# Two attention layers on one core: VectorE takes one head of two tiles per block instead of both heads of one

## The chip, the cores and the metric

The kernel runs on one core of one Trainium2 chip. The metric is the device time of one execution in microseconds. Three runs of the kernel before gave 1418.83, 1418.96 and 1419.97, median 1418.96. The profile shown is of another single execution of it, which took 1422.47 us; its span, from the first to the last instruction, is 1420.7 us.

## The reference

Two independent attention layers over 2048 tokens of width 576, with 32 heads of 18 elements each; their outputs are joined side by side.

```python
# A: one key and one value head for all 32 query heads
q = (x @ wq) as [H, S, 18];  k = x @ wk;  v = x @ wv
p = softmax(einsum("bhqd,bkd->bhqk", q, k) * 18 ** -0.5)
out_A = heads_joined(einsum("bhqk,bkd->bhqd", p, v)) @ wo

# B: per head, 4 segments of 512 tokens, causal within a segment, and a memory
for s in range(4):
    a_dot = softmax(qs @ ks.T * 18 ** -0.5 + causal) @ vs
    a_mem = (phi(qs) @ M) / (phi(qs) @ z + 1e-6)
    o = g * a_mem + (1 - g) * a_dot
    M, z = M + phi(ks).T @ vs, z + sum(phi(ks))
out_B = heads_joined(o) @ wo
```

All of A's scores are needed: 32 heads x 2048 queries x 2048 keys, so some 134 million exponentials. B has the lower triangle of 512 x 512 for each of its 4 segments and 32 heads.

## The kernel before

A first stage makes the projections of both layers, B's memory and an upper bound for each row of scores, and leaves them in DRAM. It ends about 290 us into the span. A second stage is the attention, which this change touches. A tail finishes the last output projections.

**Blocks, items, pairs.** The attention works on blocks. A block of A is 512 queries (chunk `c`) of four heads (`hg`), against all 2048 keys, as 16 key tiles `kt` of 128; a block of B is four heads in one segment, as three groups of key tiles. The four heads are two pairs `pr`. The unit of work, called a tile or an item here, is one key tile of one pair: scores of 128 keys by 2 heads by 512 queries. There are 32 blocks of A with 32 items each, and 32 blocks of B with 6 items; `after` (L869) says behind which block of A two blocks of B follow, at 13 places for A's next block.

**One item.** `scores` (L905) multiplies on TensorE into a tile `E` of two PSUM banks (three such tiles in rotation). ScalarE takes the exponential of `E` into a tile `P` in SBUF (L936). For the middle item of each turn (`copied`), VectorE first copies `E` to `W` in SBUF (L933), so that `E` is free sooner, and ScalarE reads `W`. `products` (L949) multiplies `P` by the values into `O`, accumulated over the block. Each item has two halves `hf` of 256 queries, each with both pairs.

**Exponentials on VectorE.** For the items in `BY_DVE` (L55), here key tile 0 of pair 1, VectorE makes the exponentials of both heads itself, by `exponentials` (L890): a multiply-add of the scores into an integer whose bits are read as a float (L894), two operations on its bits (L896, L897) into the tiles `n` and `q`, and four multiply-adds of a polynomial (L898 to L901), all 1024 elements wide, into the tile `PD`. The first runs with the scores; the other six wait in a list, `slow`, and one is taken per turn (L1121). A turn in which a block's last products run takes none unless it is due.

**Turns.** The order on TensorE, ScalarE and VectorE is written out by hand (L1086). The items of a block are cut into turns of three (`turns`); 32 items make ten turns of three and one of two, which is the last, turn 10. The half products are cut in the same way into `prods`, with the piece of two at place 8. In turn `k` come, in this order: the scores of turn `k` with the copy to `W`; the exponentials on ScalarE, the middle item last; eight matmuls of filling into `F` (`run_fill`, the output projection of an earlier chunk, L773, or B's memory, L829); one step of `slow` on VectorE; the products of piece `k - 2`; and what is due of the work that ends a chunk (`due`, `finish`). So the piece of two products of before runs in turn 10, the turn of two scores. Turn numbers start again in each block, and pieces 9 and 10 run in turns 0 and 1 of the block that follows. When a block's products end, VectorE copies `O` out (L975).

**Order of products.** `turn_of` (L982) holds for each pair the order in which the key tiles are multiplied. An item of VectorE is put back to the position in `LATE`, here 12 of 0 to 15, so that its exponentials are ready.

Of the kernel before, what the change touches and what calls it, by code (L numbers as in the profile page):

```python
# [8 lines left out]
F32 = mybir.dt.float32  # L9
# [3 lines left out]
U32 = mybir.dt.uint32  # L13
AF = mybir.ActivationFunctionType
# [14 lines left out]
SCALE = DH ** -0.5  # L29
# [3 lines left out]
PBUFS = 9  # L33
# [18 lines left out]
POLY = [1.0925606709321247, 32.334180715292455, 88.7610992882796, 4291.093056129828]  # L52
MANTISSA, ONE_BITS, EXPONENT = 0x7FFFFF, 0x3F800000, 0xFF800000

BY_DVE = ((0, 1),)  # L55
LATE = (12,)
QALL = [(slice(0, 36, 2), 0), (slice(1, 36, 2), 1), (slice(36, 54), 0)]
CA = 618
MZ = 126 + 32
# [15 lines left out]
def attention_pair_kernel(ctx, tc, a_xT, a_w, a_wo, b_xT, b_w, b_wo, b_beta, ident_d, hmask_d, bmask_d, cmask_d, sel_d, zmask_d, selx_d, sely_d, out):  # L75
    nc = tc.nc
# [79 lines left out]
    with ExitStack() as ph:  # L156
# [106 lines left out]
        for c in range(NCH):  # L263
# [34 lines left out]
            for t in TILES:  # L298
# [3 lines left out]
                else:  # L302

                    nm, bufs = ("nd", 2) if c == 1 and t == 4 else ("pj", 4)
# [25 lines left out]
                i = 5 * (c - 2) + TILES.index(t)  # L330
# [74 lines left out]
        for s in range(NSEG):  # L405
# [110 lines left out]
            if not last:  # L516
                e = p2.tile([128, 4, DH], F32, name="ph31")
# [92 lines left out]
    with tc.If(loose > 0, preferred_fallthrough_block=False):  # L610
        with ExitStack() as ph:
# [37 lines left out]
            with tc.For_i(0, H, 1) as h:  # L649
# [5 lines left out]
                for i in range(NKT):  # L655
                    s, j = divmod(i, 4)
                    n = 128 * (j + 1)
# [17 lines left out]
    pp = ctx.enter_context(tc.tile_pool(name="pp", bufs=1))  # L675
# [180 lines left out]
    def run_fill():  # L856

        while fill:
            key, steps = fill[0]
            if next(steps, None) is not None:  # L860
                begun.add(key)
                filled[0] += 1
                return
            fill.pop(0)
# [16 lines left out]
    def load_vseg(s):  # L881
        v = pa.tile([128, 4, H * VW + 13], F32, name="vseg", bufs=1)
        nc.sync.dma_start(v[:, :, : H * VW], vB[s].rearrange("(i p) c -> p i c", p=128))
        nc.gpsimd.memset(v[:, :, H * VW :], 0.0)
        vseg[s] = v


    slow, now = [], [0]

    def exponentials(p, e):  # L890

        y, u, w = p.bitcast(U32), pp.tile([128, 2, 512], F32, name="n", bufs=1), pp.tile([128, 2, 512], F32, name="q", bufs=1)
        v, stt = nc.vector, nc.vector.scalar_tensor_tensor
        v.tensor_scalar(y, e, EXP_A, EXP_B, op0=ALU.mult, op1=ALU.add)  # L894
        steps = [
            lambda: v.tensor_scalar(u.bitcast(U32), y, MANTISSA, ONE_BITS, op0=ALU.bitwise_and, op1=ALU.bitwise_or),  # L896
            lambda: v.tensor_scalar(w.bitcast(U32), y, EXPONENT, None, op0=ALU.bitwise_and),  # L897
            lambda: stt(p, u, POLY[0], u, op0=ALU.add, op1=ALU.mult),  # L898
            lambda: stt(p, p, POLY[1], u, op0=ALU.add, op1=ALU.mult),
            lambda: stt(p, p, POLY[2], p, op0=ALU.add, op1=ALU.mult),  # L900
            lambda: stt(p, p, POLY[3], w, op0=ALU.add, op1=ALU.mult),  # L901
        ]
        slow.extend((now[0] + 2 + i, p, step) for i, step in enumerate(steps))

    def scores(it, pr, copied):  # L905

        ab, c, hg, kt = it
        st = stacks[ab, c, hg // 2]
        h = 2 * (hg % 2) + pr
        e = psE.tile([128, 2, 512], F32, name="E")  # L910
        dve = ab == "A" and (kt, pr) in BY_DVE
        p = pp.tile([128, 2, 512], F32, name="PD" if dve else "P", bufs=1 if dve else PBUFS)
        state[it, pr] = p
        n = 512 if ab == "A" else 512 - 128 * kt if kt < 2 else 384
        if ab == "A":
            for j, r0 in enumerate(HALF):
                rows = slice(r0, r0 + KR)
                nc.tensor.matmul(e[:, j], kstA[rows, 128 * kt : 128 * kt + 128], st[rows, h, :], start=True, stop=True)  # L918
            if (kt, pr) in BY_DVE:
                exponentials(p, e)  # L920
                return lambda: None
        else:
            for k, c0 in BKEYS[kt]:
                ks = slice(128 * k, 128 * k + 128)
                for j, r0 in enumerate(HALF):
                    rows = slice(r0, r0 + KR)
                    nc.tensor.matmul(  # L927
                        e[:, j, c0 : c0 + 512 - 128 * k], st[rows, 4 + h, ks], st[rows, h, 128 * k :], start=True, stop=True
                    )
        src = e  # L930
        if copied:
            src = pp.tile([128, 2, 512], F32, name="W", bufs=2)
            nc.vector.tensor_copy(src[:, :, :n], e[:, :, :n])  # L933

        def exponential():
            nc.scalar.activation(p[:, :, :n], src[:, :, :n], AF.Exp, scale=SCALE)  # L936
            if ab == "B":

                m = len(BKEYS[kt])
                diag = p.rearrange("p a (b t) -> p a b t", t=256)[:, :, 0:m, 0:128]  # L940
                nc.gpsimd.affine_select(  # L941
                    diag, diag, pattern=[[0, 2], [0, m], [1, 128]], base=0, channel_multiplier=-1, compare_op=ALU.is_ge, fill=0.0
                )

        return exponential
# [3 lines left out]
    def products(b, m, hf):  # L949


        ab, c, hg = b
        if m == hf == 0:
            acc[0] = psO.tile([128, C], F32, name="O")
        o = acc[0]
        last = (NKT - 1 if ab == "A" else 2) == m
        for j in range(4):
            kt = turn_of[j // 2][m] if ab == "A" else m
            p = state[b + (kt,), j // 2]
            assert all(x[1] is not p for x in slow)  # L960
            k, p0, q0, n = (kt, 256 * hf, 256 * hf, 256) if ab == "A" else BHALF[kt][hf]
            if ab == "A":
                v = VA[:, VW * kt : VW * kt + 32]
            else:
                v = vseg[c][:, k, VW * (4 * hg + j) : VW * (4 * hg + j) + 32]
            nc.tensor.matmul(  # L966
                o[32 * j : 32 * j + 32, q0 : q0 + n],
                v,
                p[:, j % 2, p0 : p0 + n],
                start=m == hf == 0,  # L970
                stop=last and hf == 1,
            )
        if last and hf:
            osb = pa.tile([128, C], F32, name="oe", bufs=4)
            nc.vector.tensor_copy(osb, o)  # L975
            od = oA if ab == "A" else oB
            nc.sync.dma_start(od[c][4 * hg : 4 * hg + 4].rearrange("h r t -> (h r) t"), osb)
            return hg
        return None
# [3 lines left out]
    for pr in range(2):  # L983
        ks = [kt for kt in range(NKT) if (kt, pr) not in BY_DVE]
        for (kt, p_), pos in zip(BY_DVE, LATE):
            if p_ == pr:
# [20 lines left out]
    turns, prods = [], []  # L1007
# [71 lines left out]
    def split(n, cut):  # L1079

        sizes = [3] * (n // 3)
        if n % 3:
            sizes.insert(cut, n % 3)
        return [sum(sizes[:i]) for i in range(len(sizes) + 1)]

    with tc.manual_schedule(engines={ENG.PE, ENG.Activation, ENG.DVE}):  # L1086
# [3 lines left out]
        for n, b in enumerate(blocks):  # L1090
            ms = [m for m in range(len(its)) if block_of[m] == n]
            items = [(m, k) for m in ms for k in range(2)]
            for out_, cut in ((turns, len(items) // 3), (prods, len(items) // 3 - 2)):
                at_ = split(len(items), cut)
                out_ += [items[a:z] for a, z in zip(at_, at_[1:])]
        at(ASK + 4, 0, lambda: True, lambda k: load_qf(2))
# [13 lines left out]
        for k in range(len(turns) + 2):  # L1110
            now[0] = k
            exps = [scores(its[n], pr, i == 1) for i, (n, pr) in enumerate(turns[k])] if k < len(turns) else []
            for i in (0, 2, 1) if len(exps) == 3 else range(len(exps)):
                exps[i]()
            if memory is None:
                run_fill()
            elif k >= ASK and all(its[n][0] == "A" for n, pr in turns[k]) and next(memory, None) is None:
                memory = None

            ends = k > 1 and any(hf and its[n][3] == (NKT - 1 if its[n][0] == "A" else 2) for n, hf in prods[k - 2])  # L1120
            if slow and (slow[0][0] <= k or not ends):  # L1121
                slow.pop(0)[2]()
            for n, hf in prods[k - 2] if k > 1 else []:
                ab, c = its[n][:2]
                hg = products(its[n][:3], its[n][3], hf)
                if hg in (6, 7):
                    finish(k, ab, c, hg)
                if hg == 7 and ab == "B" and c + 1 < NSEG:
                    load_vseg(c + 1)
            due(k)  # L1130
            if k == len(turns):
                halve_w(0)
            for n, pr in turns[k] if k < len(turns) else []:
                it = its[n]
                ab = it[0]
                if pr == 0:
                    prefetch(ab, keys[ab].index((ab, it[1], it[2] // 2)) + 2)
                    if it in (("A", 0, 2, 8), ("A", 0, 5, 8)):
                        load_wo(*(("B", b_wo) if it[2] == 2 else ("A", a_wo)))
# [122 lines left out]
```

## Time and profile before

| | us |
|---|---|
| median of three runs (1418.83 to 1419.97) | 1418.96 |
| the profiled execution | 1422.47 |
| its span | 1420.7 |
| TensorE busy | 1404.0 |
| ScalarE busy | 1205.4 |
| VectorE busy | 964.4 |
| GpSimd (POOL) busy | 244.6 |

In the profile, PE is TensorE's matmuls, PEld its weight loads, ACT ScalarE, DVE VectorE, POOL GpSimd and SP the engine that issues most transfers. A row of a group gives line, engine, operation, what it writes and reads, shapes and count, then the group's busy time in us, the mean of one in ns, and after the second bar the engine's idle time just before these instructions with what ended it. A row of the timeline gives start and length in us, and in brackets an idle time and its releaser. The ends of matmuls are modelled, so that a TensorE that is held back may still count as busy. Successive instructions of ScalarE and VectorE overlap in their records; the distance from start to start is what one costs.

### The profile page before, as it was taken

How to read it: one execution, taken by the hardware profiler on the slowest of the kernel's cores; microseconds unless marked ns; L12 is line 12 of the kernel's file. 1: busy time of each engine (PE TensorE's matmuls, PEld its weight loads, DVE VectorE, ACT ScalarE, POOL GpSimd, SP SyncE). 2: the span in 40 equal slices, each digit the busy share in tenths (PEclk: the TensorE clock that was granted, in tenths of full speed). 3: DMA queues.
4: the chain of work that ended last, by engine and by line, in shares of the span. 5: the costliest groups of instructions: out<-in, count | busy, mean ns of one | idle time of the engine just before them, and what ended most of it. 6: DMA issues, size and time to landing. Idle time of an engine off the chain costs nothing.

```text
span 1420.7 us, 39951 instructions
## 1 busy us (share of the span) xinstructions
PE 1404.0 (99%) x17132; PEld 843.3 (59%) x17132; DVE 964.4 (68%) x1157; ACT 1205.4 (85%) x1447; POOL 244.6 (17%) x326
## 2 busy tenths in 40 slices
PE   9999999999999999999999999999999999999998
PEld 6788888745555555555555555555555555555558
DVE  6656456456677767776766777666767766777663
ACT  4543434479999999999999999999999999999991
POOL 2431000003313213221110160131011400100002
PEclk9999999999999999999999999999999999999999
DMA  9766546557564535332312543232104221110013
GB/s 283 253 216 188 166 146 214 174 171 214 156 214 159 165 120 166 91 109 77 110 58 70 166 128 92 62 107 80 51 34 132 67 76 44 60 45 18 9 59 112
DMA packets 90720, 172.63 MB, mean 122 GB/s; under 512 B 14576, under 2 KB 22889, under 8 KB 90110
## 3 DMA queue, kind: packets, MB, share of 16 engines
q1 hardware_dynamic: 84122, 160.01, 36.0%
q0 software_dynamic: 1664, 4.78, 1.3%
q10 hardware_dynamic: 4752, 5.24, 1.1%
q8 instruction: 135, 2.21, 0.7%
q14 instruction: 47, 0.39, 0.1%
HBM read 99.32 MB, written 70.67 MB: 120 GB/s over the span
## 4 chain that ended last, share of the span: by engine, by line
PE 68%; ACT 7%; issue 2%; DMA 1%; DVE 1%; SPq 0%; ACTq 0%; DVEq 0%
PE O L966 31%; PE E L918 20%; PE F L773 11%; ACT P L936 7%; PE E L927 3%; PE E L1163 2%; PE F L829 1%; DMA stB<-qB 0%; DVE W L933 0%; PE F L1163 0%; PE O L1163 0%; DMA oA<-oe 0%; DMA stB<-kB 0%; DMA sm<-oA 0%; SPq L696 0%
## 5 line engine op out<-in xcount | busy, mean ns | idle before, releaser
L936 ACT ACTIVATE P<-E 128x1024 f32<-128x1024 f32 (+1 forms) x800 | 780.8, 1059 | 12.7 <-PE E L918 12.3
L933 DVE COPY W<-E 128x1024 f32<-128x1024 f32 (+1 forms) x384 | 461.2, 1201 | 248.8 <-PE E L918 189.2
L966 PE MATMUL O<-P,VA 128*32 128x256 f32 x7936 | 508.8, 380 | 0.0
L936 ACT ACTIVATE P<-W 128x1024 f32<-128x1024 f32 (+1 forms) x384 | 426.3, 1110 | 3.4 <-DVE W L933 3.2
L966 PEld LDWEIGHTS O<-P,VA 128*32 128x32 f32 x7936 | 262.2, 110 | 147.6 <-issue 6.6
L918 PE MATMUL E<-stA,kstA 56*128 56x512 f32 x1920 | 329.4, 439 | 1.8 <-DVE W L933 1.1
L918 PEld LDWEIGHTS E<-stA,kstA 56*128 56x128 f32 x1920 | 154.7, 184 | 178.2 <-ACT P L936 113.7
L941 POOL TENSOR_SCALAR_AFFINE_SELECT P<-P 128x256 f32<-128x256 f32 (+1 forms) x192 | 95.0, 495 | 480.3 <-ACT P L936 446.9
L761 POOL TENSOR_TENSOR o<-o,rb 126x512 f32<-126x512 f32 (+1 forms) x55 | 79.9, 1468 | 408.9 <-DMA o<-oA 146.0
L773 PE MATMUL F<-woB,o 126*32 126x192 f32 (+1 forms) x1920 | 127.4, 338 | 0.3 <-DVE osb L797 0.3
L966 PE MATMUL O<-P,vseg 128*32 128x256 f32 (+2 forms) x1536 | 81.8, 344 | 0.8 <-issue 0.8
L773 PEld LDWEIGHTS F<-woB,o 126*32 126x32 f32 (+1 forms) x1920 | 38.2, 108 | 70.6 <-issue 63.6
L975 DVE COPY oe<-O 128x512 f32<-128x512 f32 x64 | 44.3, 692 | 41.8 <-PE O L966 41.0
L252 PE MATMUL pj<-xh,wBl 128*126 128x512 f32 x180 | 72.4, 403 | 0.0
L252 PE MATMUL pj<-xh,wBh 128*126 128x512 f32 x180 | 71.9, 400 | 0.0
L121 ACT CAST qp<-pj 126x512 fp32r<-126x512 f32 (+1 forms) x54 | 31.0, 585 | 46.1 <-DVE kmB L450 32.4
L966 PEld LDWEIGHTS O<-P,vseg 128*32 128x32 f32 x1536 | 49.1, 109 | 25.4 <-issue 2.9
L773 PE MATMUL F<-woA,o 126*32 126x192 f32 (+1 forms) x960 | 63.9, 338 | 0.0
L927 PE MATMUL E<-stB 56*128 56x256 f32 (+3 forms) x512 | 61.3, 347 | 1.4 <-ACT P L936 0.9
L122 DVE TENSOR_TENSOR qp<-pj,qp 126x512 fp32r<-126x512 f32 (+1 forms) x54 | 36.7, 685 | 35.6 <-ACT qp L121 35.3
L252 PE MATMUL pj<-xl,wBh 128*126 128x512 f32 x144 | 57.3, 399 | 0.0
L927 PEld LDWEIGHTS E<-stB 56*128 56x128 f32 x512 | 38.6, 185 | 31.1 <-ACT P L936 20.8
(194 smaller groups left out, 1387.8 us busy)
## 6 DMA issues: line engine op xcount, KB each, us to landing
stB<-kB SPq DMA_DIRECT2D x96, 144.0 KB
stB<-qB SPq DMA_DIRECT2D x32, 288.0 KB
stA<-qA SPq DMA_DIRECT2D x30, 288.0 KB
oA<-oe SPq DMA_DIRECT2D x32, 256.0 KB
oB<-oe SPq DMA_DIRECT2D x32, 256.0 KB
qA<-qp SPq DMA_DIRECT2D x16, 504.0 KB
kB<-qp SPq DMA_DIRECT2D x16, 504.0 KB
qB<-qp SPq DMA_DIRECT2D x16, 504.0 KB
```

The source lines that it names most:

```text
L121: hold(nc.scalar.copy(qp[:R, 0, :n], src))
L122: hold(nc.vector.tensor_tensor(qp[:R, 1, :n], src, qp[:R, 0, :n].bitcast(F32), op=ALU.subtract))
L252: nc.tensor.matmul(dst, w[:, c0 : c0 + M], x, start=i == 0, stop=i == len(ops) - 1)
L761: return lambda: tc.keep_in_program_order(nc.gpsimd.tensor_tensor(dst, a, b, op=op))
L773: nc.tensor.matmul(dst[32 * j : 32 * j + 32], parts[ab, c][: RT[t], t, r0 : r0 + 32], wo[ab][: RT[t], t, c0 : c0 + n], start=start, stop=stop,
L918: nc.tensor.matmul(e[:, j], kstA[rows, 128 * kt : 128 * kt + 128], st[rows, h, :], start=True, stop=True)
L927: nc.tensor.matmul(e[:, j, c0 : c0 + 512 - 128 * k], st[rows, 4 + h, ks], st[rows, h, 128 * k :], start=True, stop=True)
L933: nc.vector.tensor_copy(src[:, :, :n], e[:, :, :n])
L936: nc.scalar.activation(p[:, :, :n], src[:, :, :n], AF.Exp, scale=SCALE)
L941: nc.gpsimd.affine_select(diag, diag, pattern=[[0, 2], [0, m], [1, 128]], base=0, channel_multiplier=-1, compare_op=ALU.is_ge, fill=0.0)
L966: nc.tensor.matmul(o[32 * j : 32 * j + 32, q0 : q0 + n], v, p[:, j % 2, p0 : p0 + n], start=m == hf == 0, stop=last and hf == 1,)
L975: nc.vector.tensor_copy(osb, o)
```

## The change

`BY_DVE` names two items per block of A, key tile 0 of pair 1 (turn 0) and key tile 5 of pair 0 (turn 3). Both are middle items of their turns. Of each, VectorE makes the exponentials of the first head only, with the same seven operations, 512 wide; the second head it copies to `W`, and ScalarE takes a 512-wide exponential of it. The six steps behind the first operation are grouped in three pairs, and a pair is taken per turn. `PD` has two buffers in place of one; `n` and `q` are half as wide. The two items' products stand at positions 7 (pair 1) and 12 (pair 0). The piece of two products moves from place 8 to place 9, so that it runs in turn 0 of the block that follows.

```diff
-BY_DVE = ((0, 1),)
-LATE = (12,)
+BY_DVE = ((0, 1), (5, 0))
+LATE = (7, 12)
...
-    def exponentials(p, e):
-
-        y, u, w = p.bitcast(U32), pp.tile([128, 2, 512], F32, name="n", bufs=1), pp.tile([128, 2, 512], F32, name="q", bufs=1)
-        v, stt = nc.vector, nc.vector.scalar_tensor_tensor
+    def exponentials(p, e, whole):
+
+        u, w = (pp.tile([128, 512], F32, name=nm, bufs=1) for nm in "nq")
+        v, stt, y = nc.vector, nc.vector.scalar_tensor_tensor, p.bitcast(U32)
         v.tensor_scalar(y, e, EXP_A, EXP_B, op0=ALU.mult, op1=ALU.add)
-        steps = [
+        ops = [
...
-        slow.extend((now[0] + 2 + i, p, step) for i, step in enumerate(steps))
+        slow.extend((now[0] + 2 + i, p, ops[2 * i : 2 * i + 2], whole) for i in range(3))
...
-        p = pp.tile([128, 2, 512], F32, name="PD" if dve else "P", bufs=1 if dve else PBUFS)
+        p = pp.tile([128, 2, 512], F32, name="PD" if dve else "P", bufs=2 if dve else PBUFS)
...
-            if (kt, pr) in BY_DVE:
-                exponentials(p, e)
-                return lambda: None
+            if dve:
+                exponentials(p[:, 0], e[:, 0], p)
...
-        src = e
+        src, hs = e, slice(0, 2)
         if copied:
             src = pp.tile([128, 2, 512], F32, name="W", bufs=2)
-            nc.vector.tensor_copy(src[:, :, :n], e[:, :, :n])
+            hs = slice(1, 2) if dve else slice(0, 2)
+            nc.vector.tensor_copy(src[:, hs, :n], e[:, hs, :n])
 
         def exponential():
-            nc.scalar.activation(p[:, :, :n], src[:, :, :n], AF.Exp, scale=SCALE)
+            nc.scalar.activation(p[:, hs, :n], src[:, hs, :n], AF.Exp, scale=SCALE)
...
-            for out_, cut in ((turns, len(items) // 3), (prods, len(items) // 3 - 2)):
+            for out_, cut in ((turns, len(items) // 3), (prods, len(items) // 3 - 1)):
...
-                slow.pop(0)[2]()
+                for op in slow.pop(0)[2]:
+                    op()
```

More of the change, by code (lines that the diff above doesn't have):

```diff
@@ L959, in products @@
             p = state[b + (kt,), j // 2]
-            assert all(x[1] is not p for x in slow)
+            assert all(x[3] is not p for x in slow)
             k, p0, q0, n = (kt, 256 * hf, 256 * hf, 256) if ab == "A" else BHALF[kt][hf]
```

## The prediction

> **What bounds the kernel now.** I read the busy shares first, then the stage after 290 us by blocks, then the wait table, and last the timeline of one block, since two engines stand near full and only the timeline tells which one waits. A block is one run of 16 key tiles by two pairs (32 scored tiles) of A; a turn is three of these tiles.
>
> ```profile
> PE 1404.0 (99%) x17132; PEld 843.3 (59%) x17132; DVE 964.4 (68%) x1157; ACT 1205.4 (85%) x1447; POOL 244.6 (17%) x326
> ...
> ACT  4543434479999999999999999999999999999991
> ...
> PE 68%; ACT 7%; issue 2%; DMA 1%; DVE 1%; SPq 0%; ACTq 0%; DVEq 0%
> ...
> L936 ACT ACTIVATE P<-E 128x1024 f32<-128x1024 f32 (+1 forms) x800 | 780.8, 1059 | 12.7 <-PE E L918 12.3
> ```
>
> TensorE looks full (99%, and 68% of the chain), but the ends of its matmuls are modelled, so that a TensorE that is held back still shows as busy. ScalarE, 85% over the whole span, is at nine tenths or more in every slice of the attention stage. One block late in the stage, in the table by stretches:
>
> ```profile
> core 0: us, PE busy (x) PEld busy (x) DVE busy (x) ACT busy (x) POOL busy (x), PEclk, DMA share, GB/s
> 1204.19:1233.19 29.00, 29.00 (x410) 15.16 (x408) 20.67 (x22) 28.77 (x33) 0.00 (x0) 1.00 0.14 34
> ```
>
> A block takes 29.00 us, of which VectorE works 20.67 and ScalarE 28.77. Where the rest goes, the ScalarE timeline around a block's start shows (the number behind x is the exponentials in the piece):
>
> ```profile
> 1202.34 1.17 ACT L936 ACTIVATE P<-E 128x1024 f32<-128x1024 f32 x1
> 1203.24 1.21 ACT L936 ACTIVATE P<-W 128x1024 f32<-128x1024 f32 x1
> 1204.19 2.10 ACT L936 ACTIVATE P<-E 128x1024 f32<-128x1024 f32 x2
> 1206.52 1.94 ACT L936 ACTIVATE P<-E 128x1024 f32<-128x1024 f32 x2 [0.23 <-PE E L918]
> 1208.34 1.06 ACT L936 ACTIVATE P<-W 128x1024 f32<-128x1024 f32 x1
> 1209.29 1.94 ACT L936 ACTIVATE P<-E 128x1024 f32<-128x1024 f32 x2
> ```
>
> Successive exponentials overlap in the record, so I use start to start: one from E costs (1208.34 - 1206.52)/2 = 0.91, one from the copy W 0.95, a turn of two E and one W 2.76 (1206.52 to 1209.29). The last turn of a block (turn 10) has one E and one W, and turn 0 of the next only two E, since VectorE makes its third: 1.81. But turn 1 starts 2.33 after turn 0: ScalarE loses 0.52 there, 0.23 of it recorded as idle. The other 31 exponentials fill 28.48 of the 29.00, so this is the block's only loss.
>
> TensorE shows why it waits. A turn's order there is scores (E), eight matmuls of filling (F), then the products (O) of two turns earlier:
>
> ```profile
> 1201.12 0.73 PE L918 MATMUL E<-stA,kstA 56*128 56x512 f32 x4
> 1201.78 0.53 PE L773 MATMUL F<-woA,o 126*32 126x192 f32 x8
> ...
> 1203.11 1.18 PE L918 MATMUL E<-stA,kstA 56*128 56x512 f32 x6
> ...
> 1203.56 0.30 PEld L918 LDWEIGHTS E<-stA,kstA 56*128 56x128 f32 x4 [0.27 <-ACT P L936]
> ...
> 1205.98 0.96 PE L918 MATMUL E<-stA,kstA 56*128 56x512 f32 x6
> 1206.86 0.53 PE L773 MATMUL F<-woA,o 126*32 126x192 f32 x8
> ...
> 1208.62 0.96 PE L918 MATMUL E<-stA,kstA 56*128 56x512 f32 x6
> ...
> 1211.28 0.96 PE L918 MATMUL E<-stA,kstA 56*128 56x512 f32 x6
> ```
>
> Unheld, a full turn takes TensorE 2.65 (1208.62 to 1211.28): scores 0.89, filling and three products 1.76. In the short turn, filling and two products took 1.33 (1201.78 to 1203.11), so one product is 0.44 and the filling 0.45. A score matmul that starts at 1205.98 lets ScalarE start at 1206.52, 0.54 later. So in turn 0, where TensorE has a full turn and a score held until its buffer is free (the weight load at 1203.56; 2.87 from 1203.11 to 1205.98) and ScalarE only 1.81 of work, TensorE is late. Everywhere else ScalarE's 2.76 exceeds 2.65 and it is the bound. How often, in the wait table (total, times, longest):
>
> ```profile
> ACT P L936 <- PE E L918: 12.3, 31, 1.8
> ACT P L936 <- DVE W L933: 3.2, 8, 0.9
> ```
>
> 31 waits for 32 blocks; I count 30 of them as this one and the longest, 1.8, as another. Behind a block of B the same wait is larger:
>
> ```profile
> 640.95 0.97 PE L918 MATMUL E<-stA,kstA 56*128 56x512 f32 x6
> ...
> 641.56 1.94 ACT L936 ACTIVATE P<-E 128x1024 f32<-128x1024 f32 x2
> ...
> 643.50 0.96 PE L918 MATMUL E<-stA,kstA 56*128 56x512 f32 x6
> 644.04 1.94 ACT L936 ACTIVATE P<-E 128x1024 f32<-128x1024 f32 x2 [0.55 <-PE E L918]
> ```
>
> 2.48 from turn to turn less 1.81 is 0.67.
>
> **The change, part by part.** *ScalarE.* Two half exponentials from W (one in turn 0, one in turn 3) replace one whole W exponential of turn 3. The trace of before has no half one. Its lower bound is half a whole, 0.47, its upper the whole recorded length of a 512-wide ScalarE instruction, 0.63. I take 0.52, from the 768-wide exponentials of B:
>
> ```profile
> 639.35 1.55 ACT L936 ACTIVATE P<-E 128x768 f32<-128x768 f32 x2
> ...
> 640.73 0.91 ACT L936 ACTIVATE P<-W 128x768 f32<-128x768 f32 x1
> ```
>
> and, among the groups by line,
>
> ```profile
> L389 ACT ACTIVATE ph_e<-ph_e 126x512 f32<-126x512 f32 x28 | 17.7, 632 | 0.7
> ```
>
> A 768-wide one takes 0.69 start to start, 0.215 less than 1024, so 512 less takes 0.43 off 0.95. Per block: 2 x 0.52 - 0.95 = +0.09 (bounds 0 and +0.31).
>
> *Balance.* Turns 0 and 3 cost ScalarE 1.81 + 0.52 = 2.33 each, turn 10 stays 1.86. Before, the 1.86 and 1.81 stood side by side.
>
> *The short product turn* moves one turn on: turn 10 carries one product more on TensorE (+0.44), turn 0 of the next turn list one fewer. No product is added. Where B follows A, it falls into B's first turn in the same way; where A follows B, turn 0 carries B's products and is not shortened. The products of the two tiles that VectorE shares stand at positions 7 and 12; their exponentials end in turns 3 and 6, their first products run in turns 6 and 10, so nothing waits there. No DMA moves, and POOL issues nothing new.
>
> *Putting it together*, block behind block, on the clock of the timeline above. Turn 10's filling starts at 1201.78 as before; filling and three products take 1.76, so turn 0's scores start at 1203.54. They are not held now: the buffer that stopped them came free at 1203.56, before the second score, 0.30 after the first, needs it. Scores 0.89, filling and two products 1.33: turn 1's scores start at 1205.76, and ScalarE can have them at 1206.30. ScalarE does turn 0 from 1204.19 (scores ready 1203.54 + 0.54 = 1204.08, 0.11 to spare) for 2.33 to 1206.52. So turn 1 starts there as before, without a wait, and with half a tile more done. Turns 1 and 2 take 2.76 each, turn 3 from 1212.04 takes 2.33 to 1214.37; TensorE, 2.65 a turn from 1205.76, has turn 4's scores started at 1213.71 and ready at 1214.25, 0.12 to spare. Before, turn 4 started at 1209.29 + 2 x 2.76 = 1214.81. The rest is unchanged: 0.43 less per block (0.52 of wait less 0.09), 28.57 for 29.00.
>
> Behind B, ScalarE would finish turn 0 at 641.56 + 2.33 = 643.89 and the scores come at 644.04 as before: 0.15 of the wait stays, for 13 blocks of 32.
>
> *VectorE.* Seven 1024-wide instructions become fourteen 512-wide, ten whole copies become nine and two halves:
>
> ```profile
> L933 DVE COPY W<-E 128x1024 f32<-128x1024 f32 (+1 forms) x384 | 461.2, 1201 | 248.8 <-PE E L918 189.2 <-PE E L927 47.0 <-ACT P L936 10.6
> ...
> L898 DVE SCALAR_TENSOR_TENSOR PD<-n 128x1024 f32<-128x1024 f32 x32 | 41.5, 1296 | 0.0
> ...
> L797 DVE COPY osb<-F 128x192 f32<-128x192 f32 x72 | 25.0, 347 | 0.3 <-PE F L773 0.3
> ...
> L391 DVE SCALAR_TENSOR_TENSOR qf<-pj,ph_e 126x512 f32<-126x512 f32 x16 | 11.0, 686 | 8.7 <-ACT ph_e L389 8.6
> ```
>
> ```profile
> 1206.82 1.23 DVE L933 COPY W<-E 128x1024 f32<-128x1024 f32 x1 [0.63 <-PE E L918]
> ```
>
> Two halves by the 512-wide row are 2 x 0.69 = 1.37 for a 1024-wide step of 1.30. By the same rows a block's VectorE work grows by some 7 x 0.08 + 0.2 = 0.8 on an engine that works 20.67 of 29.00, so the total is covered. Within a turn it is tighter: copy 1.20 and a pair 1.37 are 2.57 of 2.76; in every fifth turn a copy of 0.35 brings 2.92 by recorded lengths, which overlap a little. The copy may be late by what W's exponential has to spare, about 0.3: it starts 0.84 after its turn's scores (1206.82 less 1205.98), is ready 1.23 later, and its exponential starts 2.36 after the scores (1208.34). Turn 2 had one of the two bit steps there and gets a pair of the dearer steps. I charge 0.5 us over the kernel, bounds 0 and the second rival. The Trainium skill, "VectorE: DVE Perf Modes", section "The TRN2 errata", speaks against this change: a fixed latency is paid once per instruction, so that many small tiles pay it many times; where its table has 58 cycles it measured about 150. By that, an estimate, each added instruction costs 0.16, a pair 0.16 more than the whole step of 1.30, and a turn with the copy of 0.35 would run 0.25 over ScalarE's 2.76 in two of eleven turns: 0.5 a block, less the 0.3 to spare, 0.2 x 32 = 6 us, and the sum would be near -5. The two rows above put only 2 x 0.686 - 1.296 = 0.08 on a split, half of that.
>
> **Sum.** 30 blocks have the wait, so 30 x 0.43 = -12.9; the two without it +0.2; behind B 13 x 0.15 = +2.0; VectorE +0.5: -10.2, I say -10.5 since the fixed tail also starts with five leftover products instead of six (-0.4). The profiled execution took 1422.47 around its span of 1420.7, so 1412.0 in its terms. The median of the runs shown, 1418.96, is 3.5 lower; the saving is carried over unchanged: **1408.5**.
>
> **Rivals.** *A: the wait moves.* The spare of TensorE is 0.11 at turn 0 and 0.12 at turn 4; TensorE alone needs 10 x 2.65 + 1.99 = 28.5 a block, as much as ScalarE. If 0.1 to 0.2 more is lost at one held score in each of the two turns, 30 x 0.25 comes back: -10.5 + 7.5 = -3, 1416; half of that gives 1412. For: the spare is thinner than the 0.21 (2.87 less 2.65) by which a held score lengthened turn 0. Against: no such hold is left where turn 0 now starts.
>
> *B: slower, VectorE late.* If two half steps cost 2.0 rather than 1.37, turns 2 to 6 need 1.2 + 2.0 = 3.2 of 2.76; five such turns run 2.2 behind, less the 0.3 spare, 1.9 a block instead of the 0.43 won: (1.9 - 0.43) x 32 = +47 at worst, 1466. It decides from a pair above about 1.65, where 1.2 + 1.65 is over 2.76 by 0.09 in each of five turns, 0.45 a block, and is barely slower: 1420 to 1425. For: L898's mean of 1296 ns, above the 1.2 of a copy of the same width, so that some of these steps are stretched already, and there are more instructions now. Against: the 686 ns row.
>
> *C: nothing moves,* since TensorE is the bound after all and what ScalarE saves is waited for elsewhere: 1417 to 1420. For: 68% of the chain. Against: the turns of 2.65 that stretch to ScalarE's 2.76.
>
> **How the numbers follow.** What a measurement of this kernel can tell from no change is about 0.2%, 2.8 us. Main case 0.64 (1405 to 1412), more than that since other waits of ScalarE (3.2 us on W) shrink too 0.04 (to 1403), A 0.16, C 0.07, B 0.09. Faster: main, more, and most of A, 0.82; same: C and a little of A, 0.10; slower: 0.08. The range for eight in ten runs from 1403.5 to 1416.5; it takes in A.
>
> **What would show it.** After: blocks behind blocks of about 28.57; ScalarE's wait for E from L918 down from 12.3 to 2 to 4 us, left only behind B; half exponentials 0.52 apart; halves of L898 to L901 at 0.65 to 0.69; ScalarE's wait for W near its 3.2. Wrong would be a new wait at turn 1, 4 or 0 in each block (A), waits for W above 10 us (B), or a block of 29.0 with TensorE's turns at 2.65 throughout (C).

## The result and the profile after

The changed kernel takes 1425.84 us (median of six runs, 1423.54 to 1427.26) against 1419.62 for the kernel before (six runs): a ratio of 1.0041, 95% interval 1.0028 to 1.0054. It is slower by 6 us; faster by 10.5 was forecast. The profiled execution took 1426.38 us, with a span of 1424.7.

The page of the changed kernel, its busy shares and the two groups of ScalarE's exponentials:

```profile
PE 1402.0 (98%) x17132; PEld 844.0 (59%) x17132; DVE 999.4 (70%) x1413; ACT 1208.1 (85%) x1479; POOL 238.4 (17%) x326
...
L936 ACT ACTIVATE P<-E 128x1024 f32<-128x1024 f32 (+1 forms) x800 | 792.3, 1087 | 3.7 <-PE E L918 3.4
...
L936 ACT ACTIVATE P<-W 128x1024 f32<-128x1024 f32 (+1 forms) x352 | 399.7, 1136 | 14.7 <-DVE W L933 14.1
```

The idle time of ScalarE in front of an exponential from E fell from 12.7 to 3.7 us: the wait that the change was forecast to remove is gone. In front of one from W stand 14.7 us, 14.1 of them waiting for W, where the wait table of before had 3.2. VectorE works 35 us more (999.4 for 964.4); the forecast had some 0.8 a block, 26.

Two blocks of the changed kernel, from the table by stretches, show that the loss isn't everywhere:

```profile
1181.16:1209.87 28.71, 28.71 (x412) 15.16 (x408) 21.22 (x28) 28.71 (x33) 0.00 (x0) 1.00 0.09 30
819.87:852.68 32.81, 30.10 (x410) 15.28 (x408) 28.20 (x29) 29.28 (x34) 20.48 (x14) 1.00 0.45 139
```

The columns are length, then busy time of TensorE, weight loads, VectorE, ScalarE and POOL. Where POOL is idle the block takes 28.71 instead of 29.00; 28.57 was forecast. Where POOL works 20.48 us, the block takes 32.81, and VectorE is busy 28.20 for 21.22 with one instruction more. In the kernel before, the same block (chunk 1, heads 24 to 27) took 29.35 with 22.25 us of POOL:

```profile
816.46:845.81 29.35, 29.35 (x412) 15.11 (x415) 22.24 (x21) 28.82 (x33) 22.25 (x14) 1.00 0.50 149
```

Inside that block of the changed kernel, the timelines of VectorE, of POOL and of ScalarE:

```profile
821.86 1.51 DVE L897 TENSOR_SCALAR q<-PD 128x512 uint32<-128x512 uint32 x1
...
826.30 0.68 DVE L898 SCALAR_TENSOR_TENSOR PD<-n 128x512 f32<-128x512 f32 x1
827.01 1.67 DVE L899 SCALAR_TENSOR_TENSOR PD<-PD,n 128x512 f32<-128x512 f32 x1
828.60 0.68 DVE L894 TENSOR_SCALAR PD<-E 128x512 uint32<-128x512 f32 x1
829.20 0.67 DVE L933 COPY W<-E 128x512 f32<-128x512 f32 x1
829.80 0.34 DVE L797 COPY osb<-F 128x192 f32<-128x192 f32 x1
830.06 1.56 DVE L900 SCALAR_TENSOR_TENSOR PD<-PD 128x512 f32<-128x512 f32 x1
831.66 1.65 DVE L901 SCALAR_TENSOR_TENSOR PD<-PD,q 128x512 f32<-128x512 f32 x1
833.23 1.21 DVE L933 COPY W<-E 128x1024 f32<-128x1024 f32 x1
```

```profile
821.78 1.29 POOL L761 TENSOR_TENSOR o<-o,rb 126x512 f32<-126x512 f32 x1
826.84 2.99 POOL L761 TENSOR_TENSOR o<-o,rb 126x512 f32<-126x512 f32 x2 [3.76 <-DMA rb<-rB]
829.79 2.97 POOL L761 TENSOR_TENSOR rb<-rb 126x512 f32<-126x512 f32 x2
832.72 3.20 POOL L761 TENSOR_TENSOR o<-o,rb 126x512 f32<-126x512 f32 x2
```

```profile
830.58 1.96 ACT L936 ACTIVATE P<-E 128x1024 f32<-128x1024 f32 x2
834.48 1.06 ACT L936 ACTIVATE P<-W 128x1024 f32<-128x1024 f32 x1 [1.95 <-DVE W L933]
```

A 512-wide multiply-add takes 0.68 (L898) and a bit step 0.42 (the median of L897), but here they take 1.51 to 1.67 when POOL's weighting of the outputs (L761) runs. L894, the copies to W and the copy from F, which read PSUM, keep their lengths in the same stretch. ScalarE, two exponentials of 0.905 after 830.58, was free for W at 832.39; the copy to W had only started at 833.23, and ScalarE idled 1.95.

The same over the whole kernel, from the view of single lines (shortest, median, longest in ns), first after, then before:

```profile
L899 DVE SCALAR_TENSOR_TENSOR PD<-PD,n x64: 691/692/1811, 296.7 to 1370.0; 128x512 f32<-128x512 f32 x64
L901 DVE SCALAR_TENSOR_TENSOR PD<-PD,q x64: 691/691/1664, 299.1 to 1372.4; 128x512 f32<-128x512 f32 x64
```

```profile
L899 DVE SCALAR_TENSOR_TENSOR PD<-PD,n x32: 1207/1215/2142, 302.2 to 1362.6; 128x1024 f32<-128x1024 f32 x32
L901 DVE SCALAR_TENSOR_TENSOR PD<-PD,q x32: 1206/1215/2311, 307.2 to 1367.4; 128x1024 f32<-128x1024 f32 x32
```

The longest stretch is about one microsecond for a step of 512 and for one of 1024: 1664 - 691 = 973 ns and 2311 - 1215 = 1096 ns. So the price is per step, not per element. Counting the steps L896 to L901 that took over 0.3 us longer than the median of their line: 15 before, 29 after. With smaller stretches from 0.1 us on, these add 11.5 us to VectorE before and 26.6 us after. Every one of them, 15 before and 31 after, overlaps an instruction of L761, and each is longer by what was left of that instruction when the step began, less 0.12 to 0.15 us. L897 at 821.86 is one: it took 1.09 more than its median, and the POOL instruction begun at 821.78 had 1.21 left.

### The profile page after: what moved, and what is told of

Read it like the earlier page. It is cut to its first block, busy times and chain, and to the rows that moved or that the text cites. A ratio compares the mean times of both kernels' runs of the same rounds, so it can differ in the third digit from the quotient of the medians.

```text
span 1424.7 us, 40385 instructions
## 1 busy us (share of the span) xinstructions
PE 1402.0 (98%) x17132; PEld 844.0 (59%) x17132; DVE 999.4 (70%) x1413; ACT 1208.1 (85%) x1479; POOL 238.4 (17%) x326
## 3 DMA queue, kind: packets, MB, share of 16 engines
q0 software_dynamic: 1664, 4.78, 1.4%
## 4 chain that ended last, share of the span: by engine, by line
PE 66%; DVE 6%; ACT 4%; issue 3%; DMA 1%; SPq 0%; DVEq 0%; ACTq 0%
PE O L966 30%; PE E L918 19%; PE F L773 11%; ACT P L936 4%; PE E L926 3%; DVE W L933 3%; PE E L1164 2%; PE F L829 1%; DVE PD L900 1%; DMA stB<-qB 0%; DVE sm L729 0%; DVE q L897 0%; DVE PD L898 0%; PE F L1164 0%; PE O L1164 0%
## 5 line engine op out<-in xcount | busy, mean ns | idle before, releaser
L936 ACT ACTIVATE P<-E 128x1024 f32<-128x1024 f32 (+1 forms) x800 | 792.3, 1087 | 3.7 <-PE E L918 3.4
L933 DVE COPY W<-E 128x1024 f32<-128x1024 f32 (+2 forms) x416 | 465.0, 1118 | 208.9 <-PE E L918 145.4
L936 ACT ACTIVATE P<-W 128x1024 f32<-128x1024 f32 (+1 forms) x352 | 399.7, 1136 | 14.7 <-DVE W L933 14.1
L918 PE MATMUL E<-stA,kstA 56*128 56x512 f32 x1920 | 325.1, 435 | 9.6 <-DVE W L933 8.6
L761 POOL TENSOR_TENSOR o<-o,rb 126x512 f32<-126x512 f32 (+1 forms) x55 | 78.3, 1437 | 415.8 <-DMA o<-oA 263.6
L966 PE MATMUL O<-PD,VA 128*32 128x256 f32 x512 | 71.7, 379 | 0.0
L894 DVE TENSOR_SCALAR PD<-E 128x512 uint32<-128x512 f32 x64 | 44.2, 690 | 27.9 <-PE E L918 20.4
```

Of the source, the lines that this page charges most:

```text
L761: return lambda: tc.keep_in_program_order(nc.gpsimd.tensor_tensor(dst, a, b, op=op))
L933: nc.vector.tensor_copy(src[:, hs, :n], e[:, hs, :n])
L936: nc.scalar.activation(p[:, hs, :n], src[:, hs, :n], AF.Exp, scale=SCALE)
L966: nc.tensor.matmul(o[32 * j : 32 * j + 32, q0 : q0 + n], v, p[:, j % 2, p0 : p0 + n], start=m == hf == 0, stop=last and hf == 1,)
```

## The experiments

**Theory 1**: POOL's weighting stretches VectorE's steps in SBUF, each by about one POOL instruction. The changed kernel has twice as many steps, two behind one another in a turn, and a turn with two stretched ones no longer fits, so that W comes late. **Theory 2**: VectorE is overfull by its own work. **Theory 3**: the moved product turn costs.

### POOL's weighting left out, after and before

```diff
+        if (ab, c) != blocks[-1][:2]:
+            return [lambda: None] * (3 if mem else 1)
         steps = [step(o, o, rb, ALU.mult)]
```

> The changed kernel without POOL's weighting of the outputs by the inverse sums (line 761), left out for every chunk but the last, so that the output is not normalised there. Theory 1 (POOL stretches VectorE): the steps L896 to L901 then keep their medians of 0.42 to 0.69 us everywhere, ScalarE's wait for W falls from 14.1 us to below 4, and the time is 1407 to 1413, below the unchanged kernel. Theory 2 (VectorE is overfull by itself: more instructions, pairs and the reciprocals): the wait for W stays at 10 us or more and the time at 1421 to 1426.

> The kernel before with the same weighting left out, as the yardstick for the run beside it. Theory 1: it loses its own few stretched steps, 1415 to 1419, so that the changed kernel without weighting is faster than this one by 7 to 11 us. Theory 2: the changed one stays slower than this one by 4 to 7 us.

The transfers of the weighting's tiles stay; only POOL's instructions are gone. Measured: after without weighting 1414.19, before without it 1420.35, and the unchanged kernel before 1420.40 on that chip. The sign of the change turns round: 6.2 us faster in place of 6.2 slower (1425.84 less 1419.62). The kernel before loses no time by POOL that these runs can tell (ratio 1.0005, 0.9995 to 1.0014). The changed kernel without weighting, a step and ScalarE's waits (lines are two further on):

```profile
L903 DVE SCALAR_TENSOR_TENSOR PD<-PD,q x64: 691/692/695, 300.4 to 1360.5; 128x512 f32<-128x512 f32 x64
```

```profile
ACT P L938 <- DVE W L935: 3.9, 5, 1.1
ACT P L938 <- PE E L920: 2.1, 3, 1.7
```

No step is longer than 695 ns, and 14.1 us of waiting for W have become 3.9. Theory 1 holds, theory 2 does not explain the loss. Both times lie above what was expected, by 1 us each, and the difference of 6.2 is under the 7 to 11 expected, for reasons given below.

### The two parts alone

```diff
-(prods, len(items) // 3 - 2)
+(prods, len(items) // 3 - 1)
```

> The kernel before with only the short product turn moved. By the sum of the prediction turn 1's scores start 0.22 earlier in the blocks that follow a block of A, so the wait of turn 1 falls from 0.52 to 0.30 there: 17 x 0.22 = 3.7 us less, 1415 to 1417, and VectorE's steps as before. Rival (the moved turn is what costs): 1422 or more, with new waits of ScalarE for E.

> The changed kernel with the short product turn left where it was. Theory 1: the wait for W is that of the changed kernel, about 14 us, and the wait for E of turn 1 is nearly gone too, since turn 0 of ScalarE lasts 2.33; with TensorE 0.22 later at turn 4, 1425 to 1430. If the moved turn were the cause of the loss, 1410 to 1416.

The first is the kernel before with this edit, the second the changed kernel without it. Measured: 1418.23 (ratio 0.9985, 0.9976 to 0.9995) and 1425.97 (1.0031, 1.0014 to 1.0049). Their waits, the moved turn alone first:

```profile
ACT P L936 <- PE E L918: 7.8, 13, 1.9
ACT P L936 <- DVE W L933: 3.2, 6, 1.6
```

```profile
ACT P L936 <- DVE W L933: 14.2, 19, 2.1
ACT P L936 <- PE E L918: 3.0, 4, 1.9
```

Moving the turn is good for 2 us. Start to start, it shortened the wait of turn 1 behind a block of A from 0.52 to 0.28 (0.30 was expected); about 0.065 a block came back at the next turn, so the time is 1 us above the range. The loss is all in VectorE's part. Theory 3 falls.

### POOL's instructions in halves

```diff
-            return lambda: tc.keep_in_program_order(nc.gpsimd.tensor_tensor(dst, a, b, op=op))
+            def two():
+                for h in range(2):
+                    cs = slice(256 * h, 256 * h + 256)
+                    tc.keep_in_program_order(nc.gpsimd.tensor_tensor(dst[:, cs], a[:, cs], b[:, cs], op=op))
+            return two
```

> The changed kernel with each of POOL's weighting instructions cut into two of half the width; the computation is the same. If a step of VectorE waits for POOL's running instruction to end, the longest steps fall from 1.5 to 1.8 us to about 1.0 to 1.2, ScalarE's wait for W from 14 us to 6 to 9, and the time to 1418 to 1422. Rival: if the hold lasts for POOL's work in all and not for one instruction, the longest steps stay at 1.5 or more and the time at 1424 to 1428.

> Control: the kernel before with POOL's weighting in halves. Its waits for W were 3.2 us, and without any weighting (e2) it kept its time, so 1418 to 1421. If it falls to 1415 or below, halves help by something else than the changed kernel's meetings with POOL.

Measured: on the changed kernel 1416.06 (ratio to before 0.9965, 0.9953 to 0.9978), 4.5 us less than the kernel before beside it (1420.52), where without the halves it took 6.2 more. On the kernel before 1419.70 (0.9998, 0.9989 to 1.0008): nothing. POOL's instruction and a step of VectorE, changed kernel:

```profile
L764 POOL TENSOR_TENSOR o<-o,rb x110: 722/738/1211, 429.4 to 1396.3; 126x256 f32<-126x256 f32 x88, 72x256 f32<-72x256 f32 x22
```

```profile
L906 DVE SCALAR_TENSOR_TENSOR PD<-PD,q x64: 691/692/1119, 300.1 to 1362.3; 128x512 f32<-128x512 f32 x64
```

POOL's instruction takes 0.74 where the whole one took 1.29, and the longest of this step 1.12 where it was 1.66. The number of steps stretched by over 0.3 us stays, 30 for 29, while their sum falls from 26.6 to 14.4 us. So a step waits for the POOL instruction that is running to end, not for POOL's work as a whole: 110 instructions of 0.74 are more work than 55 of 1.29. ScalarE's wait for W fell to 4.9 us, below the 6 to 9 expected, and the time to 2 us below its range.

### One step per turn in place of a pair

```diff
-LATE = (7, 12)
+LATE = (12, 14)
-        slow.extend((now[0] + 2 + i, p, ops[2 * i : 2 * i + 2], whole) for i in range(3))
+        slow.extend((now[0] + 2 + i, p, ops[i + 1 : i + 2] if i else ops[:2], whole) for i in range(5))
```

> The changed kernel with one multiply-add of 512 per turn instead of a pair (only the two short bit steps stay together), spread over turns 0 to 10, and the products at positions 12 and 14. The count of instructions is the same. If it is the pair in one turn that runs out of the turn (copy 1.14 + 0.68 + 1.66 = 3.5 of 2.76, against 1.14 + 1.66 = 2.8 alone), the wait for W falls from 14 us to 3 to 5 and the time to 1408 to 1413. Rival, the count alone: the wait for W stays at 10 us or more and the time at 1420 or more.

> Both remedies together: one multiply-add of VectorE per turn, and POOL's weighting in halves. What is left of the waits for W in e6 was 2.9 us, so at most 1 to 3 us more: 1410 to 1413. If it is no faster than e6 (1412.5 to 1414.5), the waits that are left are the reciprocals of L729 and B's memory on VectorE, not POOL.

Measured: 1413.57 (0.9948, 0.9931 to 0.9964), and with the halves as well 1410.54 (0.9937, 0.9921 to 0.9954), both faster than the kernel before and the changed one. The first lies 0.6 us above its range, the second within it. The two intervals overlap, so these runs do not show that the halves still add something to the first. The waits of the first:

```profile
ACT P L936 <- PE E L918: 3.0, 4, 1.7
ACT P L936 <- DVE W L933: 2.9, 7, 0.7
```

23 steps are still stretched, by 19.7 us in all, three quarters of the changed kernel's. But a turn that holds one of them still ends in time, and ScalarE waits 2.9 us for W instead of 14.1. So it is not the count of stretched steps that costs, but a stretched one that shares its turn with a second step.

### The two heads in one tile

A further variant makes the two heads' first steps into one tile and then takes six steps of 1024, as before the change; both tiles' products stand at position 12. The main part of its edit:

```diff
-    def exponentials(p, e, whole):
+    def exponentials(p):
-        u, w = (pp.tile([128, 512], F32, name=nm, bufs=1) for nm in "nq")
+        u, w = (pp.tile([128, 2, 512], F32, name=nm, bufs=1) for nm in "nq")
...
+                nc.vector.tensor_scalar(y[:, i].bitcast(U32), e[:, 0], EXP_A, EXP_B, op0=ALU.mult, op1=ALU.add)
+                if i:
+                    exponentials(y)
```

> The two heads of VectorE side by side in one tile: two first operations of 512, then six steps of 1024 as in the kernel before, in turns 3 to 7 (the two bit steps together); ScalarE's half exponentials and the moved turn as in the changed kernel; the copies of O have two buffers in place of four to make room. If the count of steps that meet POOL is the cost, their stretched number is that of the kernel before, the wait for W is 3 to 6 us and the time 1408 to 1414. Rival: with the steps bunched in turns 3 to 7 VectorE is late there anyway, 1418 or more.

> The two heads side by side as in e7, but the room is taken from the tiles of the weighting (8 buffers in place of 10), and the copies of O have their four buffers again. In e7 VectorE and TensorE waited for those copies' transfers; if that was its whole loss, 1409 to 1415 and no wait for oe. If the bunched steps are late by themselves, 1418 or more.

Measured: 1428.31 (1.0048, 1.0030 to 1.0065) and 1418.58 (0.9992, 0.9982 to 1.0001). Both lie above the ranges of the main expectation and where the rival, bunched steps that come late, had put them. The traces point to the room that was taken instead. In the first, from the wait table:

```profile
PE O L974 <- DVE oe L983: 12.4, 5, 6.0
...
DVE oe L983 <- DMA oA<-oe: 10.8, 2, 6.9
```

With two buffers the copies of O waited for their transfers, and TensorE for the copies. In the second only 8 steps are stretched, by 7.1 us, ScalarE waits 4.6 us for W, and from the first exponential to the last it takes 1078.9 us, as the variant with one step per turn does with 1078.8 (1087.2 before, 1091.9 after the change). So its steps are not late. It loses after that: 46.2 us from the last exponential to the end for 40.8. That the eight buffers for the weighting cause this is likely, since the first of the two, with ten of them, also has 40.8 there; no run has the eight buffers alone.

## Why the prediction was wrong

**The wait of turn 1: right.** ScalarE at a block's start, changed kernel, behind a block of A and behind one of B:

```profile
1268.58 2.02 ACT L936 ACTIVATE P<-E 128x1024 f32<-128x1024 f32 x2
1270.38 0.73 ACT L936 ACTIVATE PD<-W 128x512 f32<-128x512 f32 x1
1270.90 2.04 ACT L936 ACTIVATE P<-E 128x1024 f32<-128x1024 f32 x2
```

```profile
646.43 1.94 ACT L936 ACTIVATE P<-E 128x1024 f32<-128x1024 f32 x2
648.25 0.64 ACT L936 ACTIVATE PD<-W 128x512 f32<-128x512 f32 x1
648.92 1.94 ACT L936 ACTIVATE P<-E 128x1024 f32<-128x1024 f32 x2
```

The first turn takes 2.32 with no wait. Behind B, 648.92 - 648.25 - 0.52 = 0.15 stays, exactly the forecast 0.15. The half exponential costs 0.52, as taken.

**VectorE's term, +0.5 us: the step that failed.** Its steps were costed by the 686 ns of a 512-wide instruction and by their sum per turn; their medians are indeed 0.42 to 0.69. What it left out is that a step waits while POOL's weighting runs ("POOL issues nothing new" was as far as it looked). Under rival B it took L898's mean of 1296 ns for a sign that some steps are stretched already, but it priced neither the stretch nor its cause. The view of that line in the kernel before shows both the usual step and the long one:

```profile
L898 DVE SCALAR_TENSOR_TENSOR PD<-n x32: 1209/1215/2235, 297.8 to 1358.3; 128x1024 f32<-128x1024 f32 x32
```

The term measured: with the weighting the changed kernel takes 6.2 us more than the kernel before beside it, without the weighting 6.2 less, so some 12 us in place of 0.5; before the change, nothing that the runs can tell.

The Trainium skill, "SBUF — State Buffer", section "SBUF: two separate sides", says that VectorE and GpSimd share one pair of ports, locked for a whole instruction, when VectorE runs in a two-port mode or has two inputs in SBUF, and that the loser fully blocks. The traces agree: steps in SBUF are stretched to 1.5 to 1.8 us, copies from PSUM are not, and halving POOL's instruction halves the stretch.

The prediction cited another rule of the Trainium skill ("VectorE: DVE Perf Modes", section "The TRN2 errata"), a fixed latency per instruction, by which the sum would have been near -5. The medians of 692 for half and 1215 for whole put 0.17 on a split, close to its 0.16, where the prediction had read 0.08 off the mean of 1296. This was not where the time went: without the weighting ScalarE waits for W in 5 places only, and that the change then wins 6.2, near that rule's 5, is chance.

**The rivals.** B named the right engine and the right wait, W late, and its sign, over 10 us of it, came (14.1), but it had an even price for every pair. Its threshold, a pair above 1.65, was passed only where a step was stretched: 0.68 + 1.67 = 2.35 for such a pair, 0.68 + 0.69 for the others. The cost came in the eight blocks of A in which the weighting keeps POOL busy for 6 us or more; start to start, these take 13.2 us more in all than without the weighting, the worst 32.81. Of the other 24, all agree within 0.2 us but the first, which takes 1.1 more with POOL idle, for a cause that stays open. C did not happen. Of A a little did: the spares of 0.11 and 0.12 did not suffice everywhere, 0.05 to 0.10 is lost at turn 4 and again at the end of most blocks that follow a block of A, which makes such a block 28.71 rather than 28.57.

**What the sum would have been without POOL.** The two runs without weighting differ by 6.2 us, not 10.5. The sum held a slip besides: behind a block of B the wait was 0.67 and 0.15 of it stays, so 0.52 goes there as elsewhere and the block wins the same 0.43 (29.16 became 28.72 in the block at 641.56 before and 646.43 after). The +2.0 for these 13 blocks had no ground, and without it the prediction's terms give -12.6. Of the 6.4 us that are missing from that, start to start, some 2.4 us are the small waits just named (about 0.14 in each of the 17 blocks behind a block of A). Another 1.7 us falls at turn 7 of three blocks, where a reciprocal (L729) stands in front of a copy to W: ScalarE, ahead by the 0.43 that it won, meets the late copy and loses 1.0 to 1.3 us there for 0.5 to 0.75 before. One of them, changed kernel without weighting:

```profile
534.06 1.74 DVE L729 RECIPROCAL sm<-sm 112x256 f32<-112x256 f32 x1
535.84 0.29 DVE L732 TENSOR_SCALAR sm<-sm,omg 112x128 f32<-112x128 f32 x1
536.04 2.35 DVE L935 COPY W<-E 128x1024 f32<-128x1024 f32 x2
```

```profile
537.29 1.06 ACT L938 ACTIVATE P<-W 128x1024 f32<-128x1024 f32 x1 [1.07 <-DVE W L935]
```

The third and fourth block of A, in which VectorE also works on B's memory, took 0.41 and 0.50 more than in the kernel before without weighting, in place of 0.43 less: 1.8 us. There VectorE's own work does fill a turn, as theory 2 had it.

A gain won early in a block is given back where another engine sets the pace later in it.

## What to carry to other kernels

Steps of VectorE that work within SBUF have a second price where GpSimd works beside them, paid per instruction: look at the longest beside the median of a line before cutting it in halves, and look which of GpSimd's instructions overlap the long ones. Put such steps one at a time between instructions that read PSUM, and keep GpSimd's instructions short; here these two edits turned 1.0041 into 0.9937. When an engine's wait is removed, ask which other wait lies less than the gain behind it.

## What the runs showed of the hardware

A 512-wide and a 1024-wide step of VectorE within SBUF are stretched by the same 1.0 to 1.1 us at most, by what is left of a GpSimd instruction of 1.29; with GpSimd's at 0.74, by 0.4 to 0.6 at most. GpSimd's instructions are stretched too: those of L761 have a median of 1291 ns before the change and a longest of 2333. One short product turn moved by one place is worth 2 us by itself, though no work is saved.
